# A two-layer attention decode step: scores over four PSUM banks, and K tiles kept between the layers

## The chip, the cores and the metric

The kernel runs on one core of a Trainium2 chip. The metric is the device time of one execution in microseconds. Four runs of the kernel before took 323.35 to 325.42 us, with a median of 324.63 us. One execution was taken by the hardware profiler; all rows below are from it.

## The reference

Four sequences (batches) decode one token each. The same attention block and the same gated block are applied twice, with the same weights and the same K and V caches:

```python
x = x + A(layernorm(x), k_cache, v_cache, wq, wo)
x = x + B(layernorm(x), w_gate, w_up, w_down)
x = x + A(layernorm(x), k_cache, v_cache, wq, wo)
x = x + B(layernorm(x), w_gate, w_up, w_down)
```

A has 32 query heads and 8 K/V heads of 128 elements, and 4096 cached positions for each batch: q is x times wq, the scores are q K^T / sqrt(128), softmax over positions, times V, times wo. B is (sigmoid(x w_gate) * (x w_up)) w_down. All inputs are bf16; x has 512 elements, the gated block 1792. K and V hold 33.5 MB each and the weights 13.9 MB.

The second layer's queries depend on the first layer's full output for that batch, so K of a batch is needed twice, with the whole first layer of that batch in between, and V likewise.

## The kernel before

**Tiles and the ring.** A tile is half of one head's K or V of one batch, 128 partitions by 2048 bf16, 512 KB. Tiles live in a ring of 23 SBUF slots (`NS`, line 243). K(b,g,q) is half q of head g of batch b. All weights stay in SBUF. SyncE issues all loads in the order of a string, `order` (line 417): k is two K tiles, V is the two V tiles of one head for the first layer (l=0), v the two for the second layer (l=1), digits and letters are the weights, and r reloads K tiles listed in `again` for the batch (lines 367 and 418). V is always loaded twice, once for each layer. K(b,7,1) is loaded twice in the kernel before: released after the first layer's scores, and loaded again at r. The other 15 K tiles of a batch are held from the first layer's scores to the second's. A load waits until the slot that it takes has been read for the last time; loads are issued in order, so one that waits holds up the rest.

**Work on a batch.** `transpose_k` (line 566) transposes a K tile in place on DVE, once for each load. `scores` (line 574) makes the scores of half of the heads (s=0 or 1) in two PSUM banks, one for each q, and their last reads free the K tiles in the second layer. `softmax` (line 596) takes the maxima on DVE, the exponentials on ScalarE, turns the probabilities through the bank PT_ps, and puts them into one of four `pt_sb` buffers. `values` (line 716) multiplies them with V tiles as these land (line 728 narrow, line 684 wide) and frees them. `y_proj` (line 741) is the output projection: the heads' groups below `cut` as rows in the bank Y_ps, which ScalarE and DVE take out at lines 765 and 767 once the last of them is in, the rest as narrow products straight into PT_ps. `cross` (line 804) makes the gated block between the layers, with layer norms whose sums use the bank given by `spare` (line 711); `q_proj` and `q_spread` (lines 534 and 550) make the second layer's queries and lay them out as weights for the scores.

**The loop** (line 957) goes over batches: values and output projection of batch b in the first layer, `cross(b)`, its second-layer queries and scores, then the first-layer scores of batch b+1. Second-layer values of the batch before fill the time in between. After the last batch, `last_cross` makes the second gated block for all four batches at once.

**Order on the engines.** Nothing is written by hand: every operation is put into a list with a cost and a priority, and `place` (line 92) simulates the engines, picks among ready operations by priority, and writes each engine's order. Lower numbers come first. PS0 and PS1 are the priorities of first-layer scores, PL0 and PL1 of second-layer ones, PV0 and PV1 of the values, PK0 and PK1 of the transposes, PDEN of the softmax sums, PEV of evictions (line 545). FETCH (line 18) is the planner's cost for TensorE's crossing of a block of 256 instructions.

**PSUM.** Eight banks: three for scores (S_ps), and PT_ps, O_ps, M_ps, W_ps and Y_ps. Unit u of scores, half q, uses bank (2u + q) mod 3:

```python
bank, bkey = S_ps[(2 * u + q) % 3], f"S{(2 * u + q) % 3}"
```

Of the kernel before, what the change touches and what calls it, by code (L numbers as in the profile page):

```python
# [6 lines left out]
ACTF = mybir.ActivationFunctionType  # L7
# [7 lines left out]
LAND = 0.5  # L15
RAMP = 0.4
BLOCK = 256
FETCH = 6.1
PAIR = 0.0268
DRAIN = 0.13  # L20

# [20 lines left out]
class _Sched:  # L42
# [49 lines left out]
    def place(self):  # L92
# [15 lines left out]
        held = {}  # L108
        spi = 0
        ramp = 0  # L110
        begun, crossed = 63, -FETCH

        def slot_time(s):
            t = slot_free[s][1]
# [6 lines left out]
        def finish(o, end):  # L121
            o.end = end
            for u in o.users:
                lat = 0.03 if u.eng == o.eng and o.sem == o.eng else LAT
                u.est = max(u.est, end + (lat if o in u.deps else 0.0))
                u.left -= 1
                if u.left == 0 and u.eng != "sp":
                    pending[u.eng].append(u)

        while True:  # L130
            best = None
            for e in ENGINES:
                if e == "sp" or not pending[e]:
                    continue
                first = min(max(free_at[e], o.est) for o in pending[e])
                o = min((o for o in pending[e] if max(free_at[e], o.est) <= first + 0.05), key=lambda o: (o.prio, o.seq))
                near = [
                    p for p in pending[e]
                    if p.prio <= 0 < o.prio and max(free_at[e], p.est) <= first + min(self.look.get(e, 0.0), o.dur)
                ]  # L140
                if near:
                    o = min(near, key=lambda p: (p.est, p.seq))
                t = max(free_at[e], o.est)
                if best is None or t < best[0]:
                    best = (t, o, None)
            if spi < len(sp):
                o = sp[spi]
                if o.left == 0:
                    t, slot = max(free_at["sp"], o.est), None
                    if o.tile is not None:  # L150
                        opts = [(st, s) for s in range(self.nslots) for st in [slot_time(s)] if st is not None]
                        if opts:
                            st, slot = min(opts)
                            t = max(t, st + LAT)
                        else:
                            t = None
                    if t is not None and (best is None or t <= best[0]):
                        best = (t, o, slot)
            if best is None:
                break  # L160
            t, o, slot = best
            o.start = t
            order[o.eng].append(o)
            if o.eng == "sp":
                spi += 1
                free_at["sp"] = t + o.dur
                if o.tile is not None:
                    prev = slot_free[slot][1]
                    if prev is not None:
                        for r in prev.ops:  # L170
                            o.deps.append(r)
                        o.deps.append(prev.load)
                    o.tile.slot = slot
                    slot_free[slot] = (0.0, o.tile)
                    o.sem = f"r{slot}"
                if o.bytes:
                    b0 = max(free_at["bus"], t + START)
                    ramp = 3 if b0 > free_at["bus"] else max(ramp - 1, 0)
                    free_at["bus"] = b0 + o.bytes / (o.rate * 1e6) + (RAMP if ramp else 0.0)
                    self.bus.append((b0, free_at["bus"], o))  # L180
                    finish(o, free_at["bus"] + LAND)
                else:
                    finish(o, t + 2.5)
            else:
                pending[o.eng].remove(o)
                if o.eng == "pe":
                    n = 2 * len(o.fns)
                    to = BLOCK - begun % BLOCK
                    if n >= to:
                        at = t + o.dur * to / n  # L190
                        wait = max(0.0, crossed + FETCH - at)
                        o.dur += wait
                        crossed = at + wait
                    begun += n
                free_at[o.eng] = t + o.dur - (DRAIN if o.eng == "pe" else 0.0)
                finish(o, t + o.dur if o.sem == o.eng else t + 1.7)
# [29 lines left out]
def bass_interleave_layers__gqa_block_cached__glu_gated_glu__decode_kernel(nc, A_x, A_k, A_v, A_wq, A_wo, B_x, B_wg, B_wu, B_wd, out):  # L226
# [97 lines left out]
    M_ps = ps("M_ps", [P, 512])  # L324
    W_ps = ps("W_ps", [P, 512])
    Y_ps = ps("Y_ps", [P, 512])

    sel_p = ident_b[:].rearrange("p (g y) -> p g y", y=32)[:, :, 0:16]

# [34 lines left out]
    kt = {}  # L364
    vt = {}
    K, V = {}, {}
    again = (((7, 1),), ((7, 1),), ((7, 1),), ((7, 1),))

    def load_piece(src, q):
        t = _Tile(src)  # L370
# [43 lines left out]
        "u": lambda: load_w("wu", wu[:], B_wu.rearrange("(k p) n -> p k n", p=P), P * KD * F * 2),  # L414
        "w": load_wd,
    }
    order = 'b1kkkkk0dVkVVk23kVVVVVcaguwrvvkkkkvkkVkkVVVVVVVvvkkvvkkvrkkvvkkVVVVVVVVvvvvrkkvkkkkvvkvkVVVVVVVVvvvrvvvvvvvvvvv'
    again = (((7, 1),), ((7, 1),), ((7, 1),), ((7, 1),))
# [105 lines left out]
    def centre(o, okey, src, skey, n, mi, b, prio):  # L524
# [6 lines left out]
            ), 0.2, prio, reads=[skey, f"nm{mi}", f"cs{n}"], writes=[okey],  # L531
        )

    def q_proj(s, b, prio):
        fns = []
        n = 2 if b == 0 else 1
        for h in range(16):
            hh = 16 * s + h
            for k in range(KD):
                c0 = (hh % 8) * DH  # L540
                fns.append(mm(M_ps[:, h * n:(h + 1) * n], wq[:, hh // 8, k, c0:c0 + DH], xT[:, k, 0:n], k == 0, k == KD - 1))
        S.put("pe", fns, 0, prio, reads=["xT", f"wq{2 * s}", f"wq{2 * s + 1}"], writes=["M"])
        centre(q2T[s][:], f"q2T{s}", M_ps[:, 0:16 * n].rearrange("p (h c) -> p h c", c=n), "M", f"q{s}", 0, b, prio)

    PS0, PS1, PL0, PL1, PV0, PV1, PK0, PK1, PDEN, PEV = (1.37, -0.38, -0.4, 0.36, 1.13, 1.75, 0.42, 2.47, 1.44, -0.1)
    cnt = {"u": 0}
    turn = {"w": 0}
    pt_free = list(range(NPT))
# [25 lines left out]
    def scores(l, b, s, u, prio):  # L574
        for q in range(2):
            fns = []
            bank, bkey = S_ps[(2 * u + q) % 3], f"S{(2 * u + q) % 3}"
            for nn in range(NQ):
                for gi in range(4):
                    t = K[l, b, 4 * s + gi, q]  # L580
# [14 lines left out]

    def softmax(u, rs, rs_key, prio):
        pi = pt_free.pop(0)
        banks = [((2 * u + q) % 3) for q in range(2)]
        for q in range(2):
            S.put(  # L600
                "dve", lambda e, q=q: e.tensor_reduce(ml[:, q:q + 1], S_ps[banks[q]][:], AX.X, ALU.max, negate=True), 0.65,  # L601
                prio, reads=[f"S{banks[q]}"], writes=[f"ml{q}"],
            )
        S.put(
            "dve", lambda e: e.tensor_tensor(ml[:, 0:1], ml[:, 0:1], ml[:, 1:2], ALU.min), 0.15, prio,
# [21 lines left out]
        for q in range(2):  # L627
            S.put(
                "act", lambda e, q=q: e.activation(  # L629
                    p_sb[:, 4 * q:4 * q + 4, :].rearrange("p c x -> p (c x)"), S_ps[banks[q]][:], ACTF.Exp,  # L630
                    bias=bias, scale=rscale, accum_out=ls[:, q:q + 1],
                ), 0.8, prio, reads=[f"S{banks[q]}"] + bkey, writes=[f"p_sb{q}", f"ls{q}"],
            )
            fns = [mm(PT_ps[:, c * 64:(c + 1) * 64], p_sb[:, c, :], sel_p) for c in range(4 * q, 4 * q + 4)]
            S.put("pe", fns, 0.4, prio, reads=[f"p_sb{q}", "ident_b"], writes=["PT"])
# [74 lines left out]

    def spare():

        i = (2 * cnt["u"] + 2) % 3
        return S_ps[i], f"S{i}"

    def values(l, b, s, pi, prio, gis, narrow):

# [23 lines left out]
    def y_proj(l, s, prio, gis):  # L741

        nb = 1 if l == 0 else B
        cut = (7, 5)[l]
        y = PT_ps[:, 0:nb * KD].rearrange("p (b k) -> p b k", b=nb)

        def of(h):
# [130 lines left out]
    def spread(l, b, s, prio):  # L878
        u = cnt["u"]
        cnt["u"] += 1  # L880
        if l == 0:
            q_spread(q1T[:, 16 * s:16 * s + 16, b], f"q1T{s}", u, prio, ('act', 'dve')[0])
        else:
            q_spread(q2T[s][:], f"q2T{s}", u, prio, ('act', 'dve')[1])
        return u

    def attend(l, b, s, prio, u=None):
# [6 lines left out]
        else:  # L894
            for g, q in again[b]:
                if g // 4 == s:
                    transpose_k(1, b, g, q, (PL0, PL1)[s])
        scores(l, b, s, u, prio)
        return softmax(u, rs_q[1][:, b:b + 1] if l else None, f"rs_q1{b}", prio)

# [35 lines left out]
    def parts(narrow):  # L936
# [4 lines left out]
            return range(0, 2), range(2, 3), range(3, 4)  # L941
        return range(0, 2), range(2, 4)

    def use_later(tiles, narrow):
        while tiles:
            n = 1
# [5 lines left out]
            use(1, b, g, g + n - 1, PV1, narrow)  # L952
# [4 lines left out]
    for b in range(B):  # L957
        use_later([t for t in later[b] if t[0] == b - 1], NARROW[2])
        for s in range(NH):
            for gis in parts(NARROW[s]):  # L960
                use(0, b, 4 * s + gis[0], 4 * s + gis[-1], PV0, NARROW[s])
                y_proj(0, s, PX, gis)
        cross(b, PX)
        us = []
        for s in range(NH):
            q_proj(s, b, PX)
            us.append(spread(1, b, s, PX))
        if b < B - 1:
            us.append(spread(0, b + 1, 0, PS0))
        use_later([t for t in later[b + 1] if t[0] < b], NARROW[3])  # L970
        for s in range(NH):
            pis[1, b, s] = attend(1, b, s, (PL0, PL1)[s], us[s])
            if s == 0 and b < B - 1:
                us.append(spread(0, b + 1, 1, PS1))
        if b < B - 1:
# [45 lines left out]
```

## Time and profile before

| | |
|---|---|
| median of 4 runs | 324.63 us |
| the profiled execution | 323.66 us |
| its span, first to last instruction | 321.9 us |
| granted TensorE clock, mean | 0.634 |
| PE busy | 208.6 us (65%) |
| DVE busy | 159.7 us (50%) |
| ScalarE busy | 57.9 us (18%) |
| moved by DMA | 117.36 MB, mean 365 GB/s |
| loads of K tiles, V tiles | 68, 128 |
| K transposes on DVE (line 571) | 68, mean 1228 ns |
| score matmuls (line 584) | 512, mean 605 ns |

Busy shares are means over the whole span; the page's slices show where the load stream dips. SyncE's own waits tell what each load waited for before it was issued, and the time to landing follows the issue. PE rows overlap, since matmuls are pipelined. Idle time of an engine that is not the bound costs nothing.

### The profile page before, as it was taken

To read this page: it belongs to the slowest core of one execution; us is meant where nothing else is said; L and a number is where in the kernel's file an instruction comes from. 1 tells how busy PE (TensorE), PEld (TensorE's weight loads), DVE (VectorE), ACT (ScalarE), POOL (GpSimd) and SP (SyncE) were. 2 spreads that over 40 slices of the span, in tenths; PEclk is the share of its full clock that TensorE was granted. 3 is DMA by queue.
4 is the path that set the end of the run, shared out by engine and by line. 5 is a ranking of instruction groups with operands and counts; after the bars stand their busy time and mean duration, and the time that the engine had idled before them with its cause. 6 is when DMAs were issued, how large, how long until landed. Compare 5 with 4: busy or idle time off the path is not lost.

```text
span 321.9 us, 10756 instructions
## 1 busy us (share of the span) xinstructions
PE 208.6 (65%) x4756; PEld 138.4 (43%) x4756; DVE 159.7 (50%) x433; ACT 57.9 (18%) x142; POOL 27.1 (8%) x107
## 2 busy tenths in 40 slices
PE   0005437554469768777698586857686758789884
PEld 0003234424435334566344354744343546546574
DVE  6690535103379982066888600349987202344223
ACT  0002301300003612001046130000434300003300
POOL 5200100100001111000011010000111100001101
PEclk9999999657575555555657555556565555555755
DMA  7999999999999999999999999997999999989910
GB/s 234 391 407 388 407 396 409 382 385 378 400 316 404 411 405 409 407 408 362 318 375 413 410 406 408 406 407 274 354 411 409 408 408 409 391 305 321 410 38 3
DMA packets 37471, 117.36 MB, mean 365 GB/s; under 512 B 3376, under 2 KB 9264, under 8 KB 37424
## 3 DMA queue, kind: packets, MB, share of 16 engines
q1 hardware_dynamic: 37392, 116.67, 94.5%
q8 instruction: 37, 0.61, 0.7%
q14 instruction: 10, 0.08, 0.1%
q10 hardware_dynamic: 32, 0.00, 0.0%
HBM read 116.66 MB, written 0.00 MB: 362 GB/s over the span
## 4 chain that ended last, share of the span: by engine, by line
DMA 45%; PE 20%; SPq 15%; DVE 9%; issue 7%; ACT 3%; POOLq 0%; POOL 0%; DVEq 0%; ACTq 0%
DMA ring<-in_A_v_cache_dram 29%; DMA ring<-in_A_k_cache_dram 11%; SPq L373 10%; PE S_ps L584 8%; SPq L394 6%; DMA wu<-in_B_w_up_dram 5%; PE O_ps L728 4%; DVE ring L571 3%; PE PT_ps L335 3%; PE M_ps L335 3%; ACT p_sb L629 2%; DVE ml L601 1%; PE Y_ps L335 1%; DVE qbd L560 1%; PE W_ps L684 1%
## 5 line engine op out<-in xcount | busy, mean ns | idle before, releaser
L571 DVE STREAM_TRANSPOSE ring<-ring 128x1024 int32<-128x1024 int32 x68 | 82.4, 1228 | 21.3 <-DMA ring<-in_A_k_cache_dram 20.6
L728 PE MATMUL O_ps<-pt_sb,ring 128*128 128x4 bf16 x1856 | 61.3, 167 | 25.0 <-DMA ring<-in_A_v_cache_dram 22.7
L728 PEld LDWEIGHTS O_ps<-pt_sb,ring 128*128 128x128 bf16 x1856 | 55.4, 104 | 42.5 <-DMA ring<-in_A_v_cache_dram 26.4
L584 PE MATMUL S_ps<-ring,qbd 128*16 128x512 bf16 x512 | 57.5, 605 | 7.2 <-DVE qbd L560 3.0
L601 DVE TENSOR_REDUCE ml<-S_ps 128x1 f32<-128x512 f32 x32 | 21.4, 669 | 23.3 <-PE S_ps L584 23.3
L584 PEld LDWEIGHTS S_ps<-ring,qbd 128*16 128x16 bf16 x512 | 14.1, 114 | 30.0 <-issue 20.6
L737 DVE TENSOR_TENSOR oT<-O_ps,winv 128x12 bf16<-128x12 f32 (+1 forms) x16 | 2.5, 159 | 44.3 <-PE O_ps L728 44.3
L629 ACT ACTIVATE p_sb<-S_ps,cols 128x512 bf16<-128x512 f32 x16 | 12.3, 774 | 59.7 <-DVE cols L624 41.3
L335 PE MATMUL Y_ps<-wo,oT 128*1 128x512 bf16 x112 | 15.8, 599 | 5.8 <-DMA wo<-in_A_wo_dram 3.4
L335 PE MATMUL M_ps<-xTj,wq 128*128 128x4 bf16 x128 | 3.7, 166 | 23.9 <-DMA wq<-in_A_wq_dram 23.9
L335 PE MATMUL PT_ps<-ident_b,p_sb 128*128 128x64 bf16 x128 | 11.6, 231 | 10.9 <-ACT p_sb L629 10.8
L335 PEld LDWEIGHTS M_ps<-xT,wq 128*128 128x128 bf16 x512 | 14.2, 102 | 6.9 <-issue 4.8
L464 POOL TENSOR_TENSOR cols<-cols 128x1 f32<-128x1 f32 (+1 forms) x10 | 6.6, 656 | 122.6 <-DVE cols L508 68.3
L629 ACT ACTIVATE p_sb<-S_ps,tr 128x512 bf16<-128x512 f32 x16 | 10.9, 684 | 31.1 <-DVE tr L618 17.2
L335 PE MATMUL M_ps<-xT,wq 128*128 128x1 bf16 (+1 forms) x512 | 14.8, 165 | 2.3 <-issue 1.3
L654 POOL TENSOR_TENSOR cols<-cols 128x1 f32<-128x1 f32 x16 | 3.1, 193 | 157.2 <-ACT p_sb L629 157.2
L335 PEld LDWEIGHTS PT_ps<-ident_b,p_sb 128*128 128x128 bf16 x128 | 7.2, 116 | 16.5 <-ACT p_sb L629 15.7
L335 PEld LDWEIGHTS M_ps<-xTj,wq 128*128 128x128 bf16 x128 | 3.6, 104 | 24.0 <-issue 24.0
L649 ACT ACTIVATE pt_sb<-PT_ps 128x512 bf16<-128x512 f32 x16 | 9.5, 596 | 19.5 <-PE PT_ps L335 19.5
L335 PE MATMUL PT_ps<-p_sb,ident_b 128*32 128x128 bf16 x256 | 9.7, 296 | 3.4 <-ACT p_sb L637 3.4
L637 ACT ACTIVATE p_sb<-PT_ps 128x512 bf16<-128x512 f32 x16 | 9.6, 597 | 12.1 <-PE PT_ps L335 12.1
L765 ACT ACTIVATE p_sb<-Y_ps 128x512 bf16<-128x512 f32 x5 | 3.0, 597 | 44.6 <-PE Y_ps L335 44.6
(130 smaller groups left out, 204.1 us busy)
## 6 DMA issues: line engine op xcount, KB each, us to landing
ring<-in_A_v_cache_dram SPq DMA_DIRECT2D x128, 512.0 KB, 9.6
ring<-in_A_k_cache_dram SPq DMA_DIRECT2D x68, 512.0 KB, 9.6
wo<-in_A_wo_dram SPq DMA_DIRECT2D x4, 1024.0 KB, 9.8
wq<-in_A_wq_dram SPq DMA_DIRECT2D x4, 1024.0 KB, 17.3
wg<-in_B_w_gate_dram SPq DMA_DIRECT2D x1, 1792.0 KB, 13.8
wu<-in_B_w_up_dram SPq DMA_DIRECT2D x1, 1792.0 KB, 15.0
wd<-in_B_w_down_dram SPq DMA_DIRECT2D x1, 1792.0 KB, 18.7
p_sb<-in_A_x_dram SPq DMA_DIRECT2D x1, 4.0 KB, 1.5
```

Source lines behind the costliest of these rows:

```text
L335: return lambda e: e.matmul(o, lhsT=l, rhs=r, start=start, stop=stop)
L373: return e.dma_start(ring[t.slot], t.src.rearrange("(p t) d -> p (t d)", p=P)[:, q * TS:(q + 1) * TS])
L394: S.put("sp", lambda e: e.dma_start(o, i), 0.43, 0, writes=[key], dma=key, nbytes=nbytes, rate=rate)
L464: "pool", lambda e: e.tensor_tensor(rs, vpe[:, 0:nb], mhalf[:, 0:nb], ALU.pow), 0.6, prio,
L560: S.put("dve", lambda e, o=o, i=i: e.tensor_copy(o, i), 0.2, prio, reads=["M"], writes=[f"qbd{u % NQB}"])
L571: return e.transpose(v, v)
L584: return e.matmul(bank[32 * gi:32 * gi + 16, :], lhsT=qbd[u % NQB][:, gi, nn, :], rhs=kt[:, :, nn // 2, :, nn % 2], start=nn == 0, stop=nn ...
L601: "dve", lambda e, q=q: e.tensor_reduce(ml[:, q:q + 1], S_ps[banks[q]][:], AX.X, ALU.max, negate=True), 0.65,
L629: "act", lambda e, q=q: e.activation(p_sb[:, 4 * q:4 * q + 4, :].rearrange("p c x -> p (c x)"), S_ps[banks[q]][:], ACTF.Exp, bias=bias, sc ...
L637: "act", lambda e: e.activation(pt1.rearrange("p c g a h -> p (c g a h)"), PT_ps[:], ACTF.Copy), 0.65, prio,
L649: "act", lambda e: e.activation(pt_sb[pi][:].rearrange("p c g t h -> p (c g t h)"), PT_ps[:], ACTF.Copy), 0.65,
L728: return e.matmul(O_ps[:, gi * R:(gi + 1) * R], lhsT=ring[tile.slot][:, (t % HT) * DH:(t % HT + 1) * DH], rhs=pt_sb[pi][:, t // 4, gi, t % ...
```

## The change

K(b,7,1) is no longer loaded again: both lists `again` are empty, so r loads nothing and all 16 K tiles of a batch stay in the ring until the second layer's scores have read them. Scores rotate over four banks, S_ps 0 to 2 and Y_ps, which the output projection's rows use too; `spare` and `softmax` follow. The load order is another one. In the second layer, `cut` goes from 5 to 4. The queries of the second layer are laid out on ScalarE for s=1 of the first three batches. The last batch has its own priorities, which have the old values of PL0 and PL1; most priorities differ. The planner's costs differ: a block crossing costs FETCH and up to QUEUE more by what the load stream holds then, and an operation that follows another without a semaphore may be placed earlier. `q_rows` is a new function that is not called, since the tuple that guards it holds zeros; it is left out here.

```diff
-FETCH = 6.1
+FETCH = 2.4
+QUEUE = 3.7
...
-                u.est = max(u.est, end + (lat if o in u.deps else 0.0))
+                u.est = max(u.est, end + lat if o in u.deps else end - (DRAIN if o.eng == "pe" else 0.0))
...
-                        wait = max(0.0, crossed + FETCH - at)
+                        wait = max(0.0, ready - at)
                         o.dur += wait
-                        crossed = at + wait
+                        at += wait
+                        ready = at + FETCH + min(max(0.0, free_at["bus"] - at), QUEUE)
...
+    SB = [(S_ps[0], "S0"), (S_ps[1], "S1"), (S_ps[2], "S2"), (Y_ps, "Y")]
...
-    order = 'b1kkkkk0dVkVVk23kVVVVVcaguwrvvkkkkvkkVkkVVVVVVVvvkkvvkkvrkkvvkkVVVVVVVVvvvvrkkvkkkkvvkvkVVVVVVVVvvvrvvvvvvvvvvv'
-    again = (((7, 1),), ((7, 1),), ((7, 1),), ((7, 1),))
+    order = 'b1kkkkkV0dkVkV23VkcrVVaVVguwvvkkkkvVkkkkVVVVVVVvvkvvvkkrkkkvkvkVVVVVVVVkvvvvkkrvkkkvVvVkkVVVVVVvvvrvvvvvvvvvvvv'
+    again = ((), (), (), ())
...
-    PS0, PS1, PL0, PL1, PV0, PV1, PK0, PK1, PDEN, PEV = (1.37, -0.38, -0.4, 0.36, 1.13, 1.75, 0.42, 2.47, 1.44, -0.1)
+    PS0, PS1, PL0, PL1, PV0, PV1, PK0, PK1, PDEN, PEV = (1.82, -0.28, -0.4, 0.02, 0.83, 1.95, 2.14, 2.63, 1.34, 0.2)
+    PL, PV = [(PL0, PL1)] * (B - 1) + [(-0.4, 0.36, 1.95)[0:2]], [PV1] * B + [(-0.4, 0.36, 1.95)[2]]
...
-            bank, bkey = S_ps[(2 * u + q) % 3], f"S{(2 * u + q) % 3}"
+            bank, bkey = SB[(2 * u + q) % 4]
...
-        i = (2 * cnt["u"] + 2) % 3
-        return S_ps[i], f"S{i}"
+        return SB[(2 * cnt["u"] + 2) % 4]
...
-        cut = (7, 5)[l]
+        cut = (7, 4)[l]
...
-            q_spread(q1T[:, 16 * s:16 * s + 16, b], f"q1T{s}", u, prio, ('act', 'dve')[0])
+            q_spread(q1T[:, 16 * s:16 * s + 16, b], f"q1T{s}", u, prio, ('act', 'act', 'dve', 'act', 'dve', 'dve')[s])
...
-            q_spread(q2T[s][:], f"q2T{s}", u, prio, ('act', 'dve')[1])
+            q_spread(q2T[s][:], f"q2T{s}", u, prio, ('act', 'act', 'dve', 'act', 'dve', 'dve')[2 + s + 2 * (b == B - 1)])
```

More of the change, by code (lines that the diff above doesn't have):

```diff
@@ L110, in place @@
         ramp = 0
-        begun, crossed = 63, -FETCH
+        begun, ready = 63, 0.0
         def slot_time(s):
@@ L416, in bass_interleave_layers__gqa_block_cached__glu_gated_glu__decode_kernel @@
     }
-    order = 'b1kkkkk0dVkVVk23kVVVVVcaguwrvvkkkkvkkVkkVVVVVVVvvkkvvkkvrkkvvkkVVVVVVVVvvvvrkkvkkkkvvkvkVVVVVVVVvvvrvvvvvvvvvvv'
-    again = (((7, 1),), ((7, 1),), ((7, 1),), ((7, 1),))
+    order = 'b1kkkkkV0dkVkV23VkcrVVaVVguwvvkkkkvVkkkkVVVVVVVvvkvvvkkrkkkvkvkVVVVVVVVkvvvvkkrvkkkvVvVkkVVVVVVvvvrvvvvvvvvvvvv'
+    again = ((), (), (), ())
     k_halves = [(b, g, q) for b in range(B) for s in range(NH) for q in range(2) for g in range(4 * s, 4 * s + 4)]
@@ L532, in centre, with q_rows @@
         )
+    def q_rows(s, b, n, prio):
+        for k in range(KD):
+            fns = [
+                mm(Y_ps[32 * a:32 * a + n, :], xT[:, k, 0:n], wq[:, 2 * s + a // 2, k, (a % 2) * 512:(a % 2) * 512 + 512], k == 0, k == KD - 1)
+                for a in range(4)
+            ]
+            S.put("pe", fns, 0.43 + DRAIN, prio, reads=["xT", f"wq{2 * s + k // 2}", f"wq{2 * s + 1}"], writes=["Y"])
+        hi, lo = (pt_sb[i][:].rearrange("p g a c h -> p (g a c h)") for i in pt_free[-2:])
+        khi, klo = (f"pt{i}" for i in pt_free[-2:])
+        S.put("act", lambda e: e.activation(hi, Y_ps[:], ACTF.Copy), 0.62, prio, reads=["Y"], writes=[khi])
+        S.put("dve", lambda e: e.tensor_tensor(lo, Y_ps[:], hi, ALU.subtract), 0.65, prio, reads=["Y", khi], writes=[klo])
+        o = M_ps[:, 0:16 * n].rearrange("p (a c n) -> p a c n", a=4, n=n)
+        pick = ident_b[:].rearrange("p (a y) -> p a y", y=32)[:, :, 0:n]
+        fns = []
+        for c in range(4):
+            for x, half in enumerate((hi, lo)):
+                fns.append(mm(o[:, :, c, :], half[:, c * P:(c + 1) * P], pick, x == 0, x == 1))
+        S.put("pe", fns, 0, prio, reads=[khi, klo, "ident_b"], writes=["M"])
+        centre(q2T[s][:], f"q2T{s}", M_ps[:, 0:16 * n].rearrange("p (h c) -> p h c", c=n), "M", f"q{s}", 0, b, prio)
     def q_proj(s, b, prio):
@@ L536, in q_proj @@
         n = 2 if b == 0 else 1
+        if s == 1 and (0, 0, 0, 0)[b]:
+            return q_rows(s, b, n, prio)
         for h in range(16):
@@ L597, in softmax @@
         pi = pt_free.pop(0)
-        banks = [((2 * u + q) % 3) for q in range(2)]
+        banks = [SB[(2 * u + q) % 4] for q in range(2)]
         for q in range(2):
             S.put(
-                "dve", lambda e, q=q: e.tensor_reduce(ml[:, q:q + 1], S_ps[banks[q]][:], AX.X, ALU.max, negate=True), 0.65,
-                prio, reads=[f"S{banks[q]}"], writes=[f"ml{q}"],
+                "dve", lambda e, q=q: e.tensor_reduce(ml[:, q:q + 1], banks[q][0][:], AX.X, ALU.max, negate=True), 0.65,
+                prio, reads=[banks[q][1]], writes=[f"ml{q}"],
             )
@@ L629, in softmax @@
                 "act", lambda e, q=q: e.activation(
-                    p_sb[:, 4 * q:4 * q + 4, :].rearrange("p c x -> p (c x)"), S_ps[banks[q]][:], ACTF.Exp,
+                    p_sb[:, 4 * q:4 * q + 4, :].rearrange("p c x -> p (c x)"), banks[q][0][:], ACTF.Exp,
                     bias=bias, scale=rscale, accum_out=ls[:, q:q + 1],
-                ), 0.8, prio, reads=[f"S{banks[q]}"] + bkey, writes=[f"p_sb{q}", f"ls{q}"],
+                ), 0.8, prio, reads=[banks[q][1]] + bkey, writes=[f"p_sb{q}", f"ls{q}"],
             )
@@ L896, in attend @@
                 if g // 4 == s:
-                    transpose_k(1, b, g, q, (PL0, PL1)[s])
+                    transpose_k(1, b, g, q, PL[b][s])
         scores(l, b, s, u, prio)
@@ L942, in parts @@
         return range(0, 2), range(2, 4)
+    done = []
     def use_later(tiles, narrow):
@@ L951, in use_later @@
                 n = min(n, next(len(r) - (g % 4 - r[0]) for r in parts(narrow) if g % 4 in r))
-            use(1, b, g, g + n - 1, PV1, narrow)
+            use(1, b, g, g + n - 1, PV[len(done)], narrow)
             if b == B - 1:
@@ L963, in bass_interleave_layers__gqa_block_cached__glu_gated_glu__decode_kernel @@
         cross(b, PX)
+        done.append(b)
         us = []
         for s in range(NH):
-            q_proj(s, b, PX)
-            us.append(spread(1, b, s, PX))
+            prio = PX if s == 0 else (0, 0)[b == B - 1]
+            q_proj(s, b, prio)
+            us.append(spread(1, b, s, prio))
         if b < B - 1:
@@ L971, in bass_interleave_layers__gqa_block_cached__glu_gated_glu__decode_kernel @@
         for s in range(NH):
-            pis[1, b, s] = attend(1, b, s, (PL0, PL1)[s], us[s])
+            pis[1, b, s] = attend(1, b, s, PL[b][s], us[s])
             if s == 0 and b < B - 1:
```

## The prediction

> **What bounds the kernel now.** First the page's slices and queues, since a kernel that reads 117 MB in 322 us is bound by loads or by what holds them up.
>
> ```profile
> span 321.9 us, 10756 instructions
> PE 208.6 (65%) x4756; PEld 138.4 (43%) x4756; DVE 159.7 (50%) x433; ACT 57.9 (18%) x142; POOL 27.1 (8%) x107
> ...
> GB/s 234 391 407 388 407 396 409 382 385 378 400 316 404 411 405 409 407 408 362 318 375 413 410 406 408 406 407 274 354 411 409 408 408 409 391 305 321 410 38 3
> ...
> ring<-in_A_k_cache_dram SPq DMA_DIRECT2D x68, 512.0 KB, 9.6
> ```
>
> No engine is full. The stream runs at 405 to 413 GB/s except for the start, four dips (slices 11, 18 to 20, 27 and 28, 35 and 36) and the last two slices. Next, stretches of the trace (columns: stretch, length, busy PE, PEld, DVE, ACT, POOL, granted clock, DMA share, GB/s), a full stretch beside two dips:
>
> ```profile
> 255.00:265.00 10.00, 6.92 (x166) 4.80 (x162) 0.59 (x3) 0.76 (x2) 0.00 (x0) 0.50 1.02 406
> 216.00:228.00 12.00, 7.61 (x157) 4.84 (x157) 10.28 (x27) 1.63 (x4) 0.68 (x2) 0.64 0.83 280
> 280.00:296.00 16.00, 14.44 (x314) 9.02 (x310) 7.40 (x32) 3.12 (x7) 1.50 (x5) 0.50 0.92 312
> ```
>
> Then the queue's own waits: what SyncE waits for before it issues a load.
>
> ```profile
> SPq L373 <- PE O_ps L728: 50.5, 45, 6.0
> SPq L373 <- PE S_ps L584: 24.8, 7, 9.9
> ```
>
> It waits for slots of the ring: a value product (L728) frees a V slot, a score block (L584) frees four K slots. The single rows of the loads give the rest. In the steady stretch a tile lands every 1.278 us (V(2,0) to V(2,7): 20.45 us for 16). I call a **turn** the stretch from the landing T of a batch's last first-layer V tile to the moment R at which the first K slot of that batch is reused. T is 135.5, 199.6 and 267.2 for batches 1 to 3, and R is 155.4, 222.0 and 287.5: turns of 19.9, 22.4 and 20.3 us. In the first turn R is 91.3, with the last weight landed at 83.1. During a turn the old batch's K tiles are held, so the queue can load only as many new tiles as the other slots take. It lost about 2.6, 4.0, 4.1 and 4.1 us in the four turns, landings against 1.278 us a tile. The tail comes last:
>
> ```profile
> 308.49 0.59 PE L335 MATMUL Y_ps<-wo,q1T 128*4 128x512 bf16 x4 [0.35 <-DVE q1T L737]
> 309.02 1.01 PE L728 MATMUL O_ps<-pt_sb,ring 128*128 128x4 bf16 x32
> 309.20 0.60 ACT L765 ACTIVATE p_sb<-Y_ps 128x512 bf16<-128x512 f32 x1 [4.86 <-PE Y_ps L335]
> 309.83 0.69 DVE L767 TENSOR_TENSOR p_sb<-Y_ps,p_sb 128x512 bf16<-128x512 f32 x1 [1.40 <-ACT p_sb L765]
> 310.67 0.36 PE L335 MATMUL PT_ps<-sel_y,p_sb 128*128 128x4 bf16 x8 [0.64 <-DVE q1T L737]
> 310.88 1.42 PE L335 MATMUL PT_ps<-q1T,wo 128*128 128x4 bf16 x48
> ```
>
> The last V tile lands at 308.46, and the output projection is done at 312.30, after an eviction of the Y rows (309.20 to 310.52) that starts only when group 4 is in.
>
> **What the skill says.** The Trainium skill, "Perfetto Trace Analysis", Roofline: a lone active core may pass its share of HBM and is bounded by its 16 DMA engines at some 435 GB/s. The trace's 405 to 413 stands close below, so in full stretches only fewer bytes help. The same page, Optimization Strategy, says of gaps that repeat on the engine that should be saturated that they "can mean there isn't enough SBUF/PSUM for the next tile to be allocated"; the four dips and the two wait rows agree. The same page, Matmuls, wants independent matmul groups to rotate through PSUM banks so that evacuation overlaps. Here TensorE idles 7.2 us before all 512 score matmuls, and none of it is put down to the exponential that empties a bank. "Runtime: NRT & Kernel Launch", Instruction fetch mechanics, has code streaming in blocks of 256 instructions by the sequencer's own DMA, mostly hidden. The trace differs here: inside turns TensorE waits on nothing visible for 1.2 to 1.9 us at a time (1.78 before 275.69). I take these as such fetches behind the loads, which is inference.
>
> **The change, part by part.**
>
> *Reloads.* Four loads (68 to 64 K tiles), 4 x 1.278 = 5.1 us of stream, and four DVE transposes of 1.24 us go. The slot price: during each V phase 16 slots hold K instead of 15, so 7 instead of 8 carry V. With 3 to 6 loads in flight the before kernel still landed tiles on time (V(1,3) to V(1,7)), so I count nothing; without that cover each starved tile costs up to 1.3 us more (2.6 us apart at 97 to 100).
>
> *What a turn makes of it.* Inside a turn the queue is blocked at the end anyway, so a tile removed there is no gain by itself; what counts is how many tiles remain between R and the next T. Counting the two order strings:
> Turn 0: from R to T(1), 31 tiles before and after (13 K, 2 v, 16 V). Nothing gained.
> Turn 1: 47 tiles from T(1) to T(2), 16 issued by R, 31 left. After: 46 tiles; with 16 slots held, 7 new ones and the 10 v tiles that are used at once make 17 by R, 29 left. Two fewer, -2.6 us.
> Turn 2: 49 with 18 by R, 31 left. After: 46, and 10 + 7 = 17 by R, 29 left. -2.6 us.
> Turn 3: 29 tiles to the end, 17 by R, 12 left; three slots stood idle since the product of v(2,6) and v(2,7) came at 290.8. After: 30 tiles, of which 14 v and 7 others could be in by R: 9 to 12 left. 21 tiles fill 26.8 us, more than the turn's 20.3 and 3.6 from issue to landing, so the stream bounds the gain at about 1 us; between 0 and -1 I take -0.4.
>
> *The turns' own length.* At turn 2 a reload's transpose is on the path: the down projection ended at 212.2 and xT waited behind two transposes.
>
> ```profile
> 211.14 2.52 DVE L571 STREAM_TRANSPOSE ring<-ring 128x1024 int32<-128x1024 int32 x2 [3.24 <-DMA ring<-in_A_k_cache_dram]
> 213.58 0.18 DVE L485 SCALAR_TENSOR_TENSOR xT<-PT_ps,cols,xj 128x4 bf16<-128x4 f32 x1
> ```
>
> That is 1.1 us to win. But two K tiles now come right after the last V and may sit in the same place: 0 to -1.1, I take -0.4. Against it, two more v tiles stand in turns 1 and 3, 0.6 us of TensorE each (16 matmuls of L728) and, if TensorE waits for their landing, one tile time: +0.2 to +2.6 in all, I take +0.7.
>
> *Four banks.* No wait for a bank shows, so the rotation itself is 0; the planner may use the freedom, -1 to 0. Sharing Y means that a batch's rows can't begin before the s=1 exponential. They hardly do today: the first Y rows come at 124.7, 187.7, 254.6 and 301.6, the exponential ends at 126.0, 186.4, 252.5 and 301.2. Batch 1 would shift by 1.3 us, eight groups ahead of its use, with TensorE matmuls and further values queued behind it: 0 to +1.3, I take 0. The next unit's scores wait for L765 and L767 in turn, done by 269.8 against scores at 295: nothing.
>
> *Spreads.* s=1 of the second layer goes from DVE to ScalarE for three batches, four copies in 0.95 us against 0.92, on the idlest wide engine: 0. Without that cover 3 x 0.03.
>
> *Cut 5 to 4 in the last layer.* Four 0.6-us row matmuls, pipelined, become 16 narrow ones, and the eviction moves to group 3, ahead of the last landings. The tail's order becomes products to 309.1, 48 narrow ones of 1.42, the last oT meanwhile, 16 narrow of 0.5: done near 311.0 instead of 312.3. -1.3; between -0.5, if s=1's softmax still holds the products back, and -2.
>
> *Planner constants.* They place instructions, they run nothing: 0, with -2 to +2 for a better or worse order.
>
> Sum: -2.6 - 2.6 - 0.4 - 0.4 + 0.7 - 1.3 = -6.6 us. The profiled execution took 323.66 (span 321.9 and 1.8 around it), so 317.1 against its own time; it lies 1.0 under the median 324.63, which gives **318.0**.
>
> **Rivals.** *The reload was hidden anyway.* For it: turns 0, 2 and 3 had the reload ahead of the block, where the queue would have waited in any case. If the turns stretch by what the order gains, the tail alone is left: 323.3. Against it: the counts between R and T fall in turns 1 and 2.
>
> *Seven slots starve the stream: slower.* For it: TensorE goes 5.4 us without using a V tile in turn 3 (271.7 to 277.1), and four, then three loads were in flight after it; a V phase with one slot less can come there too. If the V phases of three batches each starve three tiles at 1.3 us, nine cost 11.7 against 6.6 gained: 329.7. It decides from six starved tiles on. Against it: 3 in flight at 280.4 still landed on time.
>
> *The turns shrink as well.* The fetch stalls (1.9 and 1.27 in turn 2, 1.78 in turn 3) and the idle slots go: another -5, 313. For it: the new fetch term. Against it: the fetches share the queue as before.
>
> That the change does not remove the loads is excluded by the diff: both lists of reloads are empty.
>
> **How the numbers follow.** Forecast, 313 to 321.5: 0.70. Hidden reload, 321.5 to 326.3: 0.15, half of it over 0.5% faster. Slower, over 326.3: 0.10. Shrunk turns, under 313: 0.05. 0.5% is 1.6 us, about what can be told from no change here, so 323.0 and 326.3 are the bounds: faster 0.83, same 0.07, slower 0.10. The range runs from 313 to 323.
>
> **What would show it.** K loads x64 and transposes x64; T(1) unchanged near 135.5; T(2) near 197; T(3) near 262, last landing near 303; from last landing to the end of the output projection 2.5 us instead of 3.8; four dips still there, with the widest at turn 2. It is wrong if turns 1 to 3 grow past 22 us, if tiles land over 1.3 us apart inside a V phase, or if score matmuls wait for a bank.

## The result, and the profile after

The changed kernel takes 322.86 us (median of 30 runs, 319.77 to 324.79) against 324.62 us of the kernel before (49 runs). The ratio is 0.9933, with an interval of 0.9917 to 0.995: 1.8 us less by the medians and 2.2 by the ratio, where 6.6 had been forecast. The ratios leave out runs over 1.5% above the fastest of the same kernel (three of these 30, 324.67 to 324.79 us), the medians keep them. The sign was right, the size was not.

The mean granted clock differs between the two profiles (0.634 before, 0.687 after), but this is not the gain: of the 30 runs the twelve with a clock under 0.65 have a mean of 322.1 us, the eighteen above it 323.1.

The page of the profiled execution after the change, the same parts as before:

```profile
span 320.9 us, 10771 instructions
PE 205.9 (64%) x4756; PEld 138.0 (43%) x4756; DVE 154.3 (48%) x418; ACT 60.3 (19%) x155; POOL 27.1 (8%) x107
...
GB/s 236 403 412 379 407 397 382 387 407 376 401 260 375 413 406 411 404 389 234 373 375 412 410 407 405 390 332 268 367 413 408 407 366 349 348 306 409 408 133 3
...
ring<-in_A_k_cache_dram SPq DMA_DIRECT2D x64, 512.0 KB, 9.7
```

The four loads are gone. But the first two dips are deeper: slices 11 and 18 (counted from 0, as in the prediction) stand at 260 and 234 GB/s, where the lowest slices of these dips were 316 and 318. The third is about as before, and the last one has become four slices long (32 to 35). The stretches from T(3), the landing of the last batch's last first-layer V tile, to the last landing at all say it in one line each (columns as in the prediction). Before, with 29 tiles to load:

```profile
267.20:308.50 41.30, 34.77 (x879) 24.75 (x880) 14.33 (x62) 7.15 (x15) 3.00 (x10) 0.54 0.93 349
```

After, with 30:

```profile
265.60:309.90 44.30, 37.02 (x971) 27.70 (x972) 14.53 (x63) 8.13 (x17) 3.00 (x10) 0.58 0.93 348
```

At 1.278 us a tile these would be 37.1 and 38.3 us. SyncE's waits, after:

```profile
SPq L376 <- PE O_ps L754: 75.7, 45, 7.2
SPq L220 <- PE S_ps L611: 25.7, 7, 10.3
SPq L220 <- DMA ring<-in_A_v_cache_dram: 19.4, 25, 3.8
SPq L376 <- PE M_ps L338: 14.1, 7, 9.7
SPq L376 <- PE W_ps L711: 10.3, 7, 3.1
SPq L376 <- PE PT_ps L338: 7.0, 10, 1.2
```

and those rows of before that the prediction does not show:

```profile
SPq L218 <- DMA ring<-in_A_v_cache_dram: 28.3, 43, 6.9
SPq L373 <- PE M_ps L335: 22.7, 11, 10.2
SPq L373 <- PE PT_ps L335: 13.9, 15, 2.1
SPq L373 <- PE W_ps L684: 13.6, 7, 4.4
```

The row of the value products went from 50.5 to 75.7 us, but the other rows together fell by as much: the six are 153.8 us before and 152.2 after. A row names the work that ended last before the wait did, which need not be what freed the slot. Sorted instead by the tile that had held the slot, which each load's semaphore tells, the waits for V slots are 118 us before and 115 after. So the sums of waiting don't show what the held tile costs; the landings do.

Added up over all tiles, what they land late (landing to landing, less 1.278 us) went from 18.3 to 25.4 us: four tiles saved 5.1 us and 7.1 us of gaps came back. A second profile with each order of loads, from the experiments below, has 20.7 us (the cut alone in the kernel before) and 25.0 us (the changed kernel again), so the growth is 4.3 to 7.1 us by these four. The last load lands at 309.92 instead of 308.46.

That the span is shorter all the same is the tail's doing. Its rows after the change:

```profile
302.01 0.60 ACT L791 ACTIVATE p_sb<-Y_ps 128x512 bf16<-128x512 f32 x1 [1.32 <-PE Y_ps L338]
302.64 0.69 DVE L793 TENSOR_TENSOR p_sb<-Y_ps,p_sb 128x512 bf16<-128x512 f32 x1 [1.39 <-ACT p_sb L791]
...
309.73 0.99 PE L754 MATMUL O_ps<-pt_sb,ring 128*128 128x4 bf16 x32
310.76 0.17 DVE L763 TENSOR_TENSOR q1T<-O_ps,winv 128x4 bf16<-128x4 f32 x1 [2.39 <-PE O_ps L754]
310.98 0.59 PE L338 MATMUL PT_ps<-q1T,wo 128*128 128x4 bf16 x16 [0.26 <-DVE q1T L763]
```

The eviction of the Y rows (302.01 to 303.33) is long past when the last tile lands at 309.92, and the projection is done at 311.57: 1.65 us after the last landing instead of 3.84. From the last landing to the end of the span it is 11.0 us instead of 13.4. The moved eviction is one part of this. The other is the s=1 softmax: its exponential ends 7.3 us before the last landing in the kernel before and 12.2 us after. Before, TensorE then works off a backlog of value products,

```profile
305.42 2.72 PE L728 MATMUL O_ps<-pt_sb,ring 128*128 128x4 bf16 x96
```

and after, from 303.7 us on, each product waits for its tile:

```profile
307.49 0.59 PE L754 MATMUL O_ps<-pt_sb,ring 128*128 128x4 bf16 x16 [0.67 <-DMA ring<-in_A_v_cache_dram]
```

### The profile page after: what moved, and what is told of

Same layout as the page of the kernel before. It is cut to its first block, busy times and chain, and to the rows that moved or that the text cites. A ratio compares the mean times of both kernels' runs of the same rounds, so it can differ in the third digit from the quotient of the medians.

```text
span 320.9 us, 10771 instructions
## 1 busy us (share of the span) xinstructions
PE 205.9 (64%) x4756; PEld 138.0 (43%) x4756; DVE 154.3 (48%) x418; ACT 60.3 (19%) x155; POOL 27.1 (8%) x107
## 4 chain that ended last, share of the span: by engine, by line
DMA 48%; PE 22%; DVE 11%; issue 9%; ACT 4%; SPq 3%; POOLq 0%; POOL 0%; DVEq 0%; ACTq 0%
DMA ring<-in_A_v_cache_dram 29%; DMA ring<-in_A_k_cache_dram 9%; DMA wq<-in_A_wq_dram 5%; PE PT_ps L338 5%; PE S_ps L611 5%; DMA wu<-in_B_w_up_dram 5%; DVE ring L598 4%; PE O_ps L754 4%; PE M_ps L338 3%; PE Y_ps L611 3%; SPq L376 3%; DVE ml L628 3%; ACT p_sb L656 2%; PE W_ps L711 1%; PE Y_ps L338 1%
## 5 line engine op out<-in xcount | busy, mean ns | idle before, releaser
L598 DVE STREAM_TRANSPOSE ring<-ring 128x1024 int32<-128x1024 int32 x64 | 77.3, 1226 | 18.5 <-DMA ring<-in_A_k_cache_dram 17.9
L754 PE MATMUL O_ps<-pt_sb,ring 128*128 128x4 bf16 x1824 | 58.8, 166 | 29.1 <-DMA ring<-in_A_v_cache_dram 21.9
L611 PE MATMUL S_ps<-ring,qbd 128*16 128x512 bf16 x384 | 42.9, 593 | 5.3 <-ACT qbd L590 2.9
L611 PEld LDWEIGHTS S_ps<-ring,qbd 128*16 128x16 bf16 x384 | 11.5, 115 | 23.3 <-issue 16.2
L628 DVE TENSOR_REDUCE ml<-S_ps 128x1 f32<-128x512 f32 x24 | 16.1, 672 | 10.0 <-PE S_ps L611 9.8
L338 PE MATMUL PT_ps<-ident_b,p_sb 128*128 128x64 bf16 x128 | 11.3, 232 | 13.6 <-ACT p_sb L656 13.4
L656 ACT ACTIVATE p_sb<-S_ps,cols 128x512 bf16<-128x512 f32 x12 | 9.3, 774 | 47.4 <-DVE cols L651 27.5
L656 ACT ACTIVATE p_sb<-S_ps,tr 128x512 bf16<-128x512 f32 x12 | 8.2, 685 | 42.3 <-DVE tr L645 22.7
L338 PEld LDWEIGHTS PT_ps<-ident_b,p_sb 128*128 128x128 bf16 x128 | 7.2, 118 | 20.6 <-ACT p_sb L656 18.5
L611 PE MATMUL Y_ps<-ring,qbd 128*16 128x512 bf16 x128 | 15.2, 623 | 0.9 <-DVE ring L598 0.9
L338 PE MATMUL Y_ps<-wo,oT 128*1 128x512 bf16 x112 | 13.9, 619 | 2.5 <-DVE oT L763 1.3
L590 ACT ACTIVATE qbd<-M_ps 32x64 bf16<-32x64 f32 x44 | 9.3, 211 | 19.2 <-PE M_ps L338 18.1
```

What stands on the lines that cost most here:

```text
L338: return lambda e: e.matmul(o, lhsT=l, rhs=r, start=start, stop=stop)
L590: "act", lambda e, o=o, i=i: e.activation(o, i, ACTF.Copy), 0.28, prio, reads=["M"], writes=[f"qbd{u % NQB}"],
L598: return e.transpose(v, v)
L611: return e.matmul(bank[32 * gi:32 * gi + 16, :], lhsT=qbd[u % NQB][:, gi, nn, :], rhs=kt[:, :, nn // 2, :, nn % 2], start=nn == 0, stop=nn ...
L628: "dve", lambda e, q=q: e.tensor_reduce(ml[:, q:q + 1], banks[q][0][:], AX.X, ALU.max, negate=True), 0.65,
L656: "act", lambda e, q=q: e.activation(p_sb[:, 4 * q:4 * q + 4, :].rearrange("p c x -> p (c x)"), banks[q][0][:], ACTF.Exp, bias=bias, scale ...
```

## The experiments

Theory, formed on these rows: a tile held between the layers costs its slot. Rivals: the new order of loads and work makes the gaps, or the gain is the tail's alone.

**The held tile and the tail, each by itself.** In the kernel before, cut alone:

```diff
-        cut = (7, 5)[l]
+        cut = (7, 4)[l]
```

> The kernel before with cut 4 instead of 5 in the last layer, nothing else. Theory: the gain of the whole change is its tail. The loads end as before (near 308.5 us) and the time from the last landing to the end of the span falls from 13.4 to about 11.0 us: 322.2 us, ratio 0.9925. Rival, the tail as the prediction sized it: 1.3 us, 323.3 us, ratio 0.996.

Measured: 323.9 us, ratio 0.9974 (0.9958 to 0.999). The tail was 12.0 us in its profile, 1.4 less, but the loads ended 2.1 us later (310.58), though the order of the work is the same up to 307 us. Worth 0.9 us, less than either account; the interval goes up to 1.4 us, so the rival's 1.3 is not excluded and the 2.4 of the theory is. In the changed kernel, the other way round:

```diff
-        cut = (7, 4)[l]
+        cut = (7, 5)[l]
```

> The changed kernel with cut 5 in the last layer, nothing else. Theory: without its tail the change is worth nothing, 325 us and ratio 1.00 against the kernel before, as the four loads saved come back as gaps between landings. Rival, reloads saved are worth something by themselves: 323.5 us or less, ratio 0.996 or less.

Measured: 323.21 us, ratio 0.9939 (0.9916 to 0.9961), against 0.9933 with it: 0.2 us, known to some 0.9 us. So the cut does not carry the gain. Its profile has a tail of 11.65 us with cut 5, still 1.75 us shorter than before, so most of the shorter tail is not the cut's: the s=1 softmax ends earlier against the last landing, and TensorE has no products left over when it comes. That part of the tail was not undone in any run; what it is worth by itself stays open.

The reload back in the changed kernel:

```diff
-    again = ((), (), (), ())
+    again = (((7, 1),), ((7, 1),), ((7, 1),), ((7, 1),))
...
-    order = 'b1kkkkkV0dkVkV23VkcrVVaVVguwvvkkkkvV...
+    order = 'b1kkkkkV0dkVkV23VkcVVaVVguwrvvkkkkvV...
```

> The changed kernel with the four K tiles loaded twice again, in its own load order (the first reload placed after the weights). Theory, slots: with 15 held tiles the value phases get the eighth slot back, the gaps between landings shrink from about 25 to about 20 us, and the four added tiles (5.1 us) are paid by that: 322 to 324.5 us. Rival, the new order and planner make the gaps and slots do not matter: gaps stay near 25 us and the time rises by 5 us to 328 us.

Measured: 322.51 us, ratio 0.9916 (0.9891 to 0.9941). Four tiles more are loaded and the time is not longer, as the theory had it. The gaps are 18.0 us instead of 25.4; of these 7.4 us, 0.5 lie before T(1), then 1.0, 3.5 and 2.4 in the three stretches from T to T and to the last landing. The stretch from 262 to 290 us, where both load the last turn's tiles, in the changed kernel:

```profile
262.00:290.00 28.00, 24.38 (x662) 18.61 (x659) 10.51 (x50) 3.52 (x8) 2.06 (x6) 0.56 0.95 336
```

and with the reload:

```profile
262.00:290.00 28.00, 22.48 (x613) 16.91 (x614) 11.25 (x49) 3.37 (x8) 1.12 (x2) 0.56 1.00 372
```

336 against 372 GB/s: one slot more in the V phase ahead of the turn, and the stream goes through. Holding the tile alone, in the kernel before:

```diff
-    again = (((7, 1),), ((7, 1),), ((7, 1),), ((7, 1),))
+    again = ((), (), (), ())
```

> The kernel before with both lists of reloads empty, its own load order and cut. Theory, slots: the four loads saved come back as gaps (18 us to 22 or 23 us), 323.5 to 325.5 us. Rival, the new order is what spoils the gain: 5 us less, 319.5 us.

Measured: 327.35 us, ratio 1.0076 (1.0055 to 1.0097). It is slower, by more than either side expected. The gaps went from 18.3 to 26.2 us, and 4.3 us are lost before the first turn already (the last weight lands at 87.4 instead of 83.1): in that order the first batch's V tiles and the weights stand behind slots that K now holds. From T(1) on, in the same order with three of the four loads saved (3.8 us), the last landing comes 172.6 us later instead of 172.9: only 0.4 us of the 3.8 are left. So the gaps come with the new order and without it.

**A slot more.** To make room for a 24th slot, five of the 14 blocks of w_down are not loaded; the products over these five use the first five blocks again. The base, still with 23 slots:

```diff
-    wd = sb("wd", [P, NF, D], bf)
+    wd = sb("wd", [P, 9, D], bf)
...
-        load_w("wd", wd[:], B_wd.rearrange("(c p) n -> p c n", p=P), P * NF * D * 2)
+        load_w("wd", wd[:], B_wd[0:9 * P, :].rearrange("(c p) n -> p c n", p=P), P * 9 * D * 2)
...
-wd[:, f, j * P:(j + 1) * P]
+wd[:, f % 9, j * P:(j + 1) * P]
```

> The changed kernel with 9 of w_down's 14 blocks loaded (the products over the last five use the first five again, so the output is not the reference's), still 23 slots. It is the base for the run with 24 slots: 0.66 MB less to load ahead of the first turn, about 1.6 us. Both theories: 321 us, ratio 0.988 to 0.990, with gaps near 25 us.

Measured: 321.76 us, ratio 0.988 (0.9836 to 0.9923), gaps 26.6 us. And with the slot:

```diff
-    NS = 23
+    NS = 24
```

> The same with a 24th slot in the ring, in the SBUF that w_down gave up; it leaves the same part of w_down out. Theory, slots: the held tile costs as it takes the slot, so a slot more gives the 7 us of gaps back, 4 us at least of them in time: 317 us or less, ratio 0.977 or less. Rival, the gaps come from the order of TensorE's work and not from slots: 321 us as with 23.

Measured: 317.21 us, ratio 0.9756 (0.9713 to 0.9799), gaps 22.0 us, last landing 304.55 instead of 309.15. The difference of the ratios is 0.0124, or 4.0 us for one slot; the intervals stand apart. The time is the theory's; of the 7 us of gaps 4.6 came back. TensorE's order differs in part between these two, since the planner places anew, so a part of the 4 us can be that.

**By turns.** The changed kernel with the reload for batches 2 and 3 only:

```diff
-    again = ((), (), (), ())
+    again = ((), (), ((7, 1),), ((7, 1),))
```

> The changed kernel with the second load of K(b,7,1) back for batches 2 and 3 alone. Theory, slots, by turns: holding costs 0.5 and 1.0 us of gaps in the first two turns and 3.5 and 2.4 in the last two, a reload 1.28 each; so this is the best of both, 321 to 322.3 us, ratio 0.988 to 0.992. Rival, turns do not tell them apart: between the two kernels, 322.5 to 322.9.

Measured: 321.93 us, ratio 0.9916 (0.9887 to 0.9945), the same as with all four. The time lies where the theory put it, but the ratio can't be told from either kernel: not decided.

**Banks.** Three banks again in the changed kernel:

```diff
-    SB = [(S_ps[0], "S0"), (S_ps[1], "S1"), (S_ps[2], "S2"), (Y_ps, "Y")]
+    SB = [(S_ps[0], "S0"), (S_ps[1], "S1"), (S_ps[2], "S2")]
...
-SB[(2 * u + q) % 4]
+SB[(2 * u + q) % 3]
```

> The changed kernel with scores over three banks again, Y kept for the output projection. Theory: no score matmul waits for a bank, so the rotation is worth nothing by itself: 322.2 to 323.6 us, ratio 0.992 to 0.997. Rival, the banks are where the shorter turns 2 and 3 come from: 324.6 us or more.

Measured: 323.51 us, ratio 0.9964 (0.9947 to 0.9981) against 0.9933: about 1.0 us for the fourth bank, at the edge of what the intervals tell. Turns 2 and 3 stay short (17.7 and 18.5 us), so the rival falls. No row of either profile shows a score matmul that waits for an exponential to empty its bank; if the 1 us is real, it comes by the order that the planner can choose; one undoing doesn't show this.

**The planner's costs.** The new costs alone in the kernel before (the first three parts of the diff above, with the starting value that belongs to them), and the old ones in the changed kernel (the same taken back):

> The kernel before with the planner's new costs alone (FETCH, QUEUE and the earlier placing of an operation that follows another without a semaphore); loads, banks, priorities and cut as before. Theory: what is left of the gain once the held tile is taken out, 2 to 3 us, is the order of work on the engines, and the costs are its largest part: 322.3 to 323.5 us, ratio 0.993 to 0.9965. Rival, the load order and the priorities make it: 324.6 us or slower, as the priorities were chosen for the old costs.

> The changed kernel with the planner's old costs, nothing else undone. Theory: turns 2 and 3 get their old length back (22 and 20 us) and the time goes to 325 us or more, ratio 1.00 or more. Rival, costs do not matter: 322.9 us, turns as in the changed kernel.

Measured: 325.89 us, ratio 1.0032 (1.0008 to 1.0056), and 324.24 us, ratio 0.9978 (0.9956 to 0.9999). Without them the changed kernel loses 1.5 us, and turn 2 is 21.0 us long instead of 19.6, in a profile that lies 2.4 us over this kernel's own median. By themselves they lose 1 us. So the first run went as its rival had it, the second as the theory had it in direction.

**The load order.** The changed kernel's order with the reload in it, in the kernel before:

```diff
-    order = 'b1kkkkk0dVkVVk23kVVVVVcaguwrvvkkkkvkkVkk...
+    order = 'b1kkkkkV0dkVkV23VkcVVaVVguwrvvkkkkvVkkkk...
```

> The kernel before with the new load order, K(b,7,1) still loaded twice (the first of them again after the weights); costs, banks, priorities and cut as before. Theory: order, costs, banks and priorities belong together, and the order alone gains under 1 us or loses: 324 to 326.5 us, ratio 0.998 to 1.006. Rival, the order is the part that makes the gain: 322.5 us, ratio 0.993.

Measured: 327.48 us, ratio 1.0098 (1.0066 to 1.0131): 3 us slower, more than expected. Turn 3 lasts 21.5 us and the tail 14.0. So neither the order nor the costs gain anything when put into the kernel before alone; the priorities were not tried alone.

**Slots where they are missing.** wq is read for the last time in the last batch's query projections, within the last turn. Eight more slots of the ring were laid into it, each free once the projection that reads it is done:

```diff
+    for i in range(4):
+        flat = wq[:, i].rearrange("p k n -> p (k n)")
+        ring += [flat[:, j * TS:(j + 1) * TS] for j in range(2)]
...
+        if b == B - 1:
+            for i in range(4):
+                t = _Tile(None)
+                t.ops, t.load = [op], S.last_write[f"wq{2 * s + i // 2}"]
+                S.extra.append(t)
```

> The changed kernel whose ring gets eight more slots in the SBUF of wq, four after the last batch's query projection of s=0 and four after that of s=1, as wq is not read any more then. Theory, slots: the last turn's gaps of 6 us shrink by half or more, since four slots come some 6 us before the first K slot does: 318.5 to 321 us, ratio 0.981 to 0.989. Rival, the last turn is bound by the s=1 softmax and not by loads: 322.9 us, tail longer by what the loads end earlier.

> The same eight slots in the kernel that loads K(b,7,1) again for batches 2 and 3. Theory, slots: there the last turn has 3.8 us of gaps and one tile more, so 319.5 to 321.5 us, ratio 0.984 to 0.990, not better than with the tile held. Rival: no gain, 322 us.

Measured: 320.38 us, ratio 0.9837 (0.98 to 0.9875), and 322.35 us, ratio 0.992 (0.9894 to 0.9946). The second is no gain on the mixed kernel: there the rival was right. The first beats both kernels. But its profile has the last turn as long as ever (44.1 us from T(3) to the last landing) and its lead ahead of it, where the order of the work is that of the changed kernel. It was therefore taken apart, with the changed kernel beside it: the first four slots alone, and the last four alone (`and s == 0`, `and s == 1` in the condition).

> The changed kernel as it is, beside the next two on the same chip, as a measure for them: 322.9 us, ratio 0.9933.

> The changed kernel with only the four slots that the query projection of s=0 frees in the last batch. Theory, slots: these come 6 us before the first K slot and carry the whole gain of the eight, so as with eight: 320 to 321 us, ratio 0.984 to 0.989, with fewer gaps in the last turn. Rival, the profile of the kernel with eight slots shows the last turn as long as before (44.1 against 44.3 us from T to the last landing), so slots there do nothing and the 2.5 us were another chip's: the same as the changed kernel beside it.

> The changed kernel with only the four slots that the query projection of s=1 frees. They come after the first K slots, when the queue is full again. Both theories: the same as the changed kernel beside it, within 1 us.

Measured on one chip: 323.34 us, ratio 0.9894 (0.9832 to 0.9957) for the changed kernel as it is; 320.46 us, ratio 0.9864 (0.9828 to 0.99) with the first four; 322.14 us, ratio 0.9881 (0.9833 to 0.9929) with the last four. In six runs each these can't be told apart among themselves. The profiles can. From T(3) to the last landing, the changed kernel:

```profile
265.60:309.70 44.10, 35.77 (x979) 28.14 (x976) 14.44 (x63) 8.12 (x17) 3.02 (x10) 0.62 0.93 348
```

with the first four slots:

```profile
263.90:305.60 41.70, 36.56 (x975) 28.31 (x973) 14.55 (x63) 8.13 (x17) 3.02 (x10) 0.54 0.97 367
```

The same 30 tiles take 2.4 us less; the five profiles of this order without the early slots have 44.0 to 44.3 us. The loads into these slots stand in SyncE's rows:

```profile
275.98 1.87 SPq L380 DMA_DIRECT2D wq<-in_A_v_cache_dram  x4
```

They go out at 276, 6.7 us before the first K slot of that batch is free (282.7), so 21 tiles are issued by then instead of 17. With the last four alone the stretch stays at 44.0 us. Against the kernel before, both versions with the early slots are faster by 1.4 to 1.6%; against the changed kernel's ratio over 30 runs (0.9917 to 0.995) their intervals stand below. How much of it the last turn makes stays open: one profile with the four early slots shows 2.4 us there, and the one with eight, which has the same four, shows nothing.

## Why the prediction was wrong in size

**The slot price failed.** Its step was: "With 3 to 6 loads in flight the before kernel still landed tiles on time (V(1,3) to V(1,7)), so I count nothing". Those rows have five to seven in flight; that three are enough was taken from one tile. How late a tile lands by the number of other loads in flight when it is issued, over the profiles of eight of these kernels (the two, and those with the reload back, the tile held in the old kernel, 24 slots, the mixed reloads, three banks and eight slots in wq):

| in flight at issue | loads | mean late, us |
|---|---|---|
| 1 | 8 | 1.59 |
| 2 | 52 | 0.90 |
| 3 | 108 | 0.39 |
| 4 | 180 | 0.14 |
| 5 | 204 | 0.06 |
| 6 and more | 949 | 0.02 |

With one V slot less the queue enters each turn thinner: the last four tiles of the last V phase were issued with 7, 7, 7 and 7 in flight before, and with 5, 5, 5 and 3 after. With the reload back it is 6, 6, 6 and 6, and with the 24th slot 7, 6, 6 and 6. Then the gated block comes, in which TensorE frees few slots: between 268.5 and 279.5 us the queue issued five loads before and four after. The drought is the same, the cover is not, and the queue runs down to two or three. This is the rival "seven slots starve the stream", in another place: it looked for starved tiles in the V phases; the late ones come behind T, in the turns. The gaps grew by 7.1 us, more than the 5.1 us of loads that were saved. The signs that the prediction had named did not tell of it: the turns stayed under 22 us, no score waited for a bank, and inside the V phases only single tiles came late (the second of V(1,0), 2.58 us after the first).

**The tile counts between R and T** failed by the same slots. "10 v tiles that are used at once make 17 by R, 29 left": measured 16 and 30 in turn 1, 15 and 31 in turn 2. For turn 3 it was "9 to 12 left", and 13 were. The v tiles are not used at once, and an unused one holds a slot. The stretches from T to T became 0.45 and 1.83 us shorter (63.67 and 65.77 us), where 2.6 had been put down for each, and that from T(3) to the last landing became 3.0 us longer, where -0.4 had been put down. T(1) came at 136.2, close to the forecast; T(2) came at 199.9 instead of 197, T(3) at 265.6 instead of 262, the last landing at 309.9 instead of 303. Half of this miss arose in the last stretch.

**The turns' own length** went better than forecast: 20.3, 19.6 and 18.3 us instead of 19.9, 22.4 and 20.3, where -0.4 and +0.7 had been put down. Turns 2 and 3 together are 4.8 us shorter. The stream gained less by it: in turn 2 three tiles fewer had been issued by R than before, and in turn 3 as many as before, but six of the 17 only in the last 4.4 us, after the queue had run down.

**The cut** was probably oversized: 0.2 us in the changed kernel and 0.9 in the kernel before, for 1.3. The interval in the kernel before still just reaches 1.3. The tail itself shrank more than forecast (2.4 us): the prediction knew the s=1 softmax only as something that might still hold the products back, and it came earlier.

**The planner's constants and the banks** had been put down as nothing, between -2 and +2 and between -1 and 0. Undone by themselves they cost 1.5 and 1.0 us. With the cut's 0.2 and the held tile's -0.5 that makes 2.2, the size of the gain. The agreement proves little: each term is known to 0.8 to 1.0 us, effects of single undoings need not add up, and the load order, the priorities and the spreads on ScalarE were not undone by themselves in the changed kernel. So where the gain comes from is open in part. As far as the runs show, the sign came out right by terms that the prediction had put at nothing, while the reloads that it counted on brought nothing; that was luck.

**The hidden-reload rival** expected that the turns stretch; they shrank. It had the right time (323.3) by luck. A hidden load leaves a gap when it goes, too, so the runs do not fully part the two accounts. But it leaves no more than its own time, 5.1 us for the four, against 7.4 us of gaps between the changed kernel and the same with the reload back; and it does not thin the queue ahead of the turn.

## What to carry to other kernels

Before a saved load is counted, ask what holds its bytes meanwhile: in a full ring a tile that stays is a slot that the stream lacks. Here one slot more was worth 4 us, and the four saved loads, 5.1 us of transfer, saved nothing that could be measured. Read how many loads are in flight when each is issued, not only whether the next one landed on time, and look for space that is dead in the stretch that starves, as wq was here. Costs, order and priorities of a planner that were chosen together can't be priced one by one: two of them lose when they are put into the old kernel alone.

## What the hardware showed

In these profiles a load of 512 KB landed on time only with some five others in flight when it was issued: it was 0.06 us late on the mean with five, 0.39 with three and 0.90 with two, most of a tile's own 1.278 us. The loads behind a late one came at the usual 1.28 us again and no closer, so what was lost was not made up. That is more gradual than the "on time or starved" the prediction had reckoned with.

Single executions of the same order of work differed by up to 4.4 us at one and the same point (T(3) at 265.6 in the changed kernel and 261.2 with the eight slots, which only act later). A profile shows where time goes in one execution; what a change is worth needs the medians.
